# Halves for GpSimd, and thresholds on ScalarE, in a kernel of attention and two feed-forward blocks

## The chip, the cores and the metric

The kernel runs on one core of one Trainium2 chip. A core has five engines that work through queues of their own: TensorE (PE, matrix products and transposes into PSUM banks), VectorE (DVE), ScalarE (ACT), GpSimd (POOL) and SyncE (SP, which here issues nearly all transfers). Each queue is worked through in order; an instruction that needs a result of another engine waits at the head of its queue, and all behind it waits too. The metric is the time of one launch in microseconds (us) on the device; lower is better.

## The reference

```python
def _attn_ref(q, k, v, tau):                       # (4, 8, 576, 64) each
    scores = scale * np.matmul(q, k.transpose(0, 1, 3, 2))
    thresh = np.max(scores, axis=-1, keepdims=True) - tau
    scores = np.where(scores >= thresh, scores, -1000000000.0)
    scores = scores - np.max(scores, axis=-1, keepdims=True)
    attn = np.exp(scores)
    attn = attn / (np.sum(attn, axis=-1, keepdims=True) + 1e-09)
    return np.matmul(attn, v).astype(np.float32)
...
x = np.ascontiguousarray(attn_out.transpose(0, 2, 1, 3)).reshape(B * S, H * D)
h = x @ w_in                                       # 2304 x 512 by 512 x 2048
g = np.where(pos, h, np.where(neg, 0.0, (h + beta) ** 2 / (4.0 * beta)))
x = g @ w_out
h2 = x @ w_in2
return (h2 * np.clip(h2 + 3.0, 0.0, 6.0) / 6.0) @ w_out2
```

## The kernel before

**Attention.** The 32 heads are worked on in 16 jobs of two heads (four jobs for each of the four batches). A job has five blocks of queries: four of 128 rows, whose scores of the two heads fill two pairs of PSUM banks, and a last one of the 64 remaining rows of both heads. For a block, TensorE makes the scores (L328). VectorE copies them out of PSUM with their sign changed and takes the minimum of each row on the way (L341, `nm`); that frees the banks. ScalarE makes the exponential, one instruction for each head (L353, `e`). VectorE adds tau to the minima (L356, the threshold `th`, two columns, one in the last block) and multiplies `e` with the comparison against the threshold, summing on the way (L362, the mask). TensorE turns the masked block (L277), ScalarE copies the turned pieces out (L390, L393, L404, L408, `Gf` and `Gt`), and TensorE multiplies them with v (L426); ScalarE copies the product to `xu` (L432).

A job's sums are inverted on VectorE (L445, L446), written to DRAM and read back spread over the partitions (`rb`, L467 two large transfers, L469 two small ones). GpSimd then multiplies `xu` with `rb` (L481). Queries and keys of jobs 4 to 15 are turned on VectorE (L286, L302), and GpSimd scales the queries (L288, `qt`).

**Feed-forward products.** Each 32-bit operand is split into a high and a low part, so that each product takes three matrix products (L666, L728, L708). For the activations ScalarE copies the high part (L649 `xh`, L683 `gh`) and VectorE or GpSimd subtracts (L650 `xl`, L684 `gl`). For the weights, which arrive as 64-bit words, eight instructions on three engines make 32-bit values: ScalarE L118 and L121, GpSimd L122, VectorE L129 and L135, GpSimd L137 (an integer addition), ScalarE L139 (high part), GpSimd L141 (low part). All are 128 x 512.

**Order.** Once the first batch's four jobs are done, a generator deals out pieces of the first feed-forward block between the pieces of attention (`mode["att"]` is true as long as attention runs, `mode["mlp"]` from the first product on); the rest follows when attention has ended. The order in which instructions of one engine stand is not that of the code: the framework schedules the program by a timeline of its own, so another length or another engine of one instruction can move its neighbours. Waits are placed by the regions that are read and written: who reads only the first 256 columns of `xu` waits for the instruction that writes these.

Of the kernel before, what the change touches and what calls it, by code (L numbers as in the profile page):

```python
# [10 lines left out]
ACTF = mybir.ActivationFunctionType  # L11
ALU = mybir.AluOpType
U32 = mybir.dt.uint32
I32 = mybir.dt.int32
# [4 lines left out]
def kernel(  # L19
# [13 lines left out]
    V, S, G, T = nc.vector, nc.scalar, nc.gpsimd, nc.tensor  # L33
    NB, NH, SEQ, D = q.shape
# [29 lines left out]
    taus = const.tile([128, 4], F32, name="taus")  # L64
# [9 lines left out]
    def f32(ap):  # L74
        return ap.bitcast(F32)
# [26 lines left out]
    def after(ins, prev, sync=False):  # L102
        if prev is not None:
            kind = mybir.DependencyClass.Sync if sync else mybir.DependencyClass.NoSync
            why = mybir.DependencyReason.ANTI if sync else mybir.DependencyReason.DATA
            tc.add_manual_dep(ins.ins, prev.ins.name, mybir.DependencyInfo(kind, why), reason="pace")

    pe_pins = []
    pins = {"S": None, "V": None, "G": None}

    def split_a(kind, m, f):
        t = wraw.pop((kind, m, f))
        pool = wbase if f < NF1 else wpool[f]
        hi = pool.tile([128, 512], F32R, tag=f"w{kind}h{f}", name=f"w{kind}h{f}")
        lo = pool.tile([128, 512], F32R, tag=f"w{kind}l{f}", name=f"w{kind}l{f}")
        c = stage.tile([128, 512], U32, tag="w_c", name="w_c", bufs=2)
        r = t[:, :, 0].bitcast(I32)
        x = S.activation(out=r, in_=t[:, :, 0], func=ACTF.Copy, scale=2.0 ** -29)  # L118
        after(x, pins["S"])
        if mode["att"]:  # L120
            after(S.activation(out=f32(c), in_=f32(t[:, :, 1]), func=ACTF.Abs), x)  # L121
            G.tensor_scalar(  # L122
                out=f32(c), in0=f32(c), scalar1=122879.9921875, scalar2=2.0 ** -15, op0=ALU.min, op1=ALU.max)
        else:
            S.activation(out=f32(c), in_=f32(t[:, :, 1]), func=ACTF.Abs)
            x = V.tensor_scalar(
                out=f32(c), in0=f32(c), scalar1=2.0 ** -15, scalar2=122879.9921875, op0=ALU.max, op1=ALU.min)
            after(x, pins["V"])
        V.tensor_scalar(out=c, in0=c, scalar1=3, scalar2=0x3FFFFFFF,  # L129
                        op0=ALU.logical_shift_left, op1=ALU.bitwise_and)  # L130
        wc[kind, m, f] = (hi, lo, c, t, r)

    def split_b(kind, m, f):
        hi, lo, c, t, r = wc.pop((kind, m, f))
        V.scalar_tensor_tensor(out=c, in0=t[:, :, 1], scalar=0xC0000000, in1=c,  # L135
                               op0=ALU.bitwise_and, op1=ALU.bitwise_or)
        x = G.tensor_tensor(out=c.bitcast(I32), in0=c.bitcast(I32), in1=r, op=ALU.add)  # L137
        after(x, pins["G"])
        x = S.activation(out=hi, in_=f32(c), func=ACTF.Copy)  # L139
        after(x, pins["S"])  # L140
        x = G.tensor_tensor(out=lo, in0=f32(c), in1=f32(hi), op=ALU.subtract)  # L141
        after(x, pins["G"])
        wsp[kind, m, f] = (hi, lo)

    wc = {}
# [61 lines left out]
    mode = {"mlp": False, "att": True, "step": False, "t": 0, "s": 0, "n": 0}  # L207
# [4 lines left out]
    qt, kt = {}, {}  # L212
# [17 lines left out]
    def load_q(j):  # L230
        if j >= NJ:
            return
        E = nc.sync if j else nc.scalar
        b, hp = jobs[j]
        for h in HEADS:
            src = q[b, 2 * hp + h]
            if j >= JT:
                strips(qn, 0, src, h)
                continue
            E.dma_start(out=qn[:, 0:4, h * D:(h + 1) * D], in_=rows(src, b))  # L240
            E.dma_start(out=qn[0:TAIL, 4, h * D:(h + 1) * D], in_=src[MAIN:SEQ, :])
# [39 lines left out]
    def unit_q(j):  # L281
        if j >= NJ or j in qt:
            return
        qt[j] = ap.tile([128, SEQ], F32, tag="qt", name="qt", bufs=2)
        if j >= JT:
            V.transpose(out=qt[j], in_=qn.rearrange("p c n -> p (c n)")[:, 0:SEQ])  # L286
            load_q(j + 1)
            G.tensor_scalar(out=qt[j], in0=qt[j], scalar1=taus[:, 1:2], scalar2=None, op0=ALU.mult)  # L288
            return
        tm = unit_bank().rearrange("p e n -> p (e n)")  # L290
        for c in range(5):
            turn(tm[:, c * 128:(c + 1) * 128], qn[:, c, :], c == 0)
        load_q(j + 1)
        reads(S.activation(out=qt[j], in_=tm[:, 0:SEQ], func=ACTF.Copy, scale=taus[:, 1:2]))
# [52 lines left out]
    def em_exp(j, i, x):  # L347
        p, nm, th, es = blk[j, i]
        n = 1 if i == NBLK - 1 else 2
        if x >= n:  # L350
            return
        e = ap.tile([128, 2, HS], F32, tag="e", name="e", bufs=3)
        pins["S"] = S.activation(out=e, in_=p[:, x], func=ACTF.Exp, bias=nm[:, x:x + 1], scale=-1.0)  # L353
        es.append(e)
        if x == n - 1:
            V.tensor_scalar(out=th[:, 0:n], in0=nm[:, 0:n], scalar1=taus[:, 0:1], scalar2=None, op0=ALU.add)  # L356

    def em_mask(j, i):
# [112 lines left out]
    def em_norm(j):  # L471
        if j not in rbs:
            return
        while any(x[0] == j for x in pvq):
            pv_chunk()
        b, hp = jobs[j]
        rz, rb = rbs.pop(j)
        if j in OVER:
            load_v(j + 2)
            x = xu.pop(j)  # L480
            G.tensor_tensor(out=x, in0=x, in1=rb, op=ALU.mult)  # L481
            done_jobs.add(j)
            if b < NB - 1:
                nc.sync.dma_start(out=xd[b][:, hp, :], in_=x[:, 0:MAIN])
            nc.sync.dma_start(out=xd[NB][:, hp, b * TAIL:(b + 1) * TAIL], in_=x[:, MAIN:SEQ])
            return
        bm = unit_bank().rearrange("p e n -> p (e n)")
        for c in range(4):
            T.transpose(bm[:, c * 128:(c + 1) * 128], rb[:, c].rearrange("p h n -> p (h n)"), ident)
        load_v(j + 2)  # L490
        bt = bm[:, 512:640]
        T.transpose(bt, rz[:, 8, :].to_broadcast([128, 128]), ident)
        x = xu.pop(j)
        reads(V.tensor_tensor(out=x[:, 0:MAIN], in0=x[:, 0:MAIN], in1=bm[:, 0:MAIN], op=ALU.mult))
        done_jobs.add(j)
        if b < NB - 1:
            nc.sync.dma_start(out=xd[b][:, hp, :], in_=x[:, 0:MAIN])
        for h in HEADS:
            r = slice(64 * h, 64 * h + 64)
            reads(V.tensor_tensor(out=x[r, MAIN:SEQ], in0=x[r, MAIN:SEQ], in1=bt[r, 64 * h:64 * h + 64], op=ALU.mult))  # L500
        nc.sync.dma_start(out=xd[NB][:, hp, b * TAIL:(b + 1) * TAIL], in_=x[:, MAIN:SEQ])
# [288 lines left out]
    while o < len(outs):  # L790
        n = len(steps)
# [138 lines left out]
    for _ in attention():  # L930
# [11 lines left out]
        while credit > 0:  # L942
            c = next(part1)
# [98 lines left out]
```

## Time and profile before

| | |
|---|---|
| median of three runs | 1124.85 us (1124.29 to 1128.67) |
| the profiled execution | 1126.53 us, span 1124.7 us |
| granted TensorE clock in it | 0.994 of full speed |
| busy: PE, DVE, ACT, POOL | 1086.1, 586.9, 614.3, 435.5 us |
| chain that ended last | PE 86%, DVE 6%, ACT 3%, DMA 2% |

A profile shows one execution. Busy time is the union of an engine's instructions in a stretch; an instruction that waits for a port or a lock after it has started counts as busy. A row by lines has: line, engine, operation, output and inputs by the program's names with their shapes, number of instructions, then busy us and mean ns of one, then idle time of the engine before them and what ended it. A row of waits says who waited for whom, the sum in us, how often, and the longest. A row of the timeline has its start and length in us, and in brackets the idle time of the engine before it. `DVE_READ_ACCUMULATOR` rows belong to the instruction before them.

### The profile page before, as it was taken

Reading aid. Unit: us, or ns where it says so; the run is one execution under the profiler, and the core shown is the slowest. Engines: PE = TensorE matmul, PEld = TensorE weight load, DVE = VectorE, ACT = ScalarE, POOL = GpSimd, SP = SyncE. Lnnn points to the kernel's source line nnn. Section 1 sums busy time; section 2 is a strip of 40 time slices with the busy share of each in tenths; the row PEclk is TensorE's granted clock in tenths of the full one; section 3 lists DMA queues with packets and bytes.
Section 4 is the critical chain, followed back from the end, with each engine's and each line's share of the span. In section 5 each row is a group of like instructions: output and inputs, shape, how many; then the busy total and the mean of one; then the engine's idle time right before and its main releaser. Section 6 shows DMA issues by size and latency. Waiting matters only on the chain.

```text
span 1124.7 us, 17618 instructions
## 1 busy us (share of the span) xinstructions
PE 1086.1 (97%) x6478; PEld 881.8 (78%) x6478; DVE 586.9 (52%) x1204; ACT 614.3 (55%) x1215; POOL 435.5 (39%) x382
## 2 busy tenths in 40 slices
PE   7988779999999999999999999999999999999998
PEld 5555557778887778888889888888888888898886
DVE  5788979876666666256535855657410211211111
ACT  5677777776666666565657766645422322333222
POOL 1133667632212221246636666568622222222221
PEclk9999999999999999999999999999999999999999
DMA  6353535433222210015322444543110110010001
GB/s 166 95 117 79 135 102 157 121 73 87 63 59 64 55 39 24 12 49 169 94 85 85 132 147 153 153 128 102 35 38 1 34 38 1 10 38 6 14 1 38
DMA packets 140422, 84.26 MB, mean 75 GB/s; under 512 B 99632, under 2 KB 123440, under 8 KB 140336
## 3 DMA queue, kind: packets, MB, share of 16 engines
q1 hardware_dynamic: 138976, 82.84, 26.8%
q8 instruction: 51, 0.84, 0.3%
q10 hardware_dynamic: 1360, 0.30, 0.1%
q14 instruction: 35, 0.29, 0.1%
HBM read 65.73 MB, written 17.37 MB: 74 GB/s over the span
## 4 chain that ended last, share of the span: by engine, by line
PE 86%; DVE 6%; ACT 3%; DMA 2%; issue 1%; POOL 1%; SPq 1%; ACTq 0%; DVEq 0%; POOLq 0%
PE Q L666 35%; PE P L708 28%; PE Q L728 7%; PE P L328 6%; PE Q L426 5%; PE Q L277 5%; DVE p L341 2%; DVE p L362 2%; ACT e L353 1%; DMA qn<-in_q_dram 1%; DMA w_raw<-in_moe_w_in_dram 0%; DMA rb<-rd 0%; DVE w_c L135 0%; ACT Gf L390 0%; SPq L227 0%
## 5 line engine op out<-in xcount | busy, mean ns | idle before, releaser
L684 POOL TENSOR_TENSOR gl<-r,gh 128x512 fp32r<-128x512 f32 (+1 forms) x190 | 202.4, 1065 | 508.3 <-ACT gh L683 506.4
L666 PE MATMUL Q<-xh,wih 128*128 128x512 f32 (+1 forms) x760 | 262.7, 346 | 6.9 <-DVE r L677 6.0
L666 PE MATMUL Q<-xh,wil 128*128 128x512 f32 (+1 forms) x760 | 257.6, 339 | 0.0
L666 PE MATMUL Q<-xl,wih 128*128 128x512 f32 (+1 forms) x760 | 257.5, 339 | 0.0
L680 DVE SCALAR_TENSOR_TENSOR r<-r,Q 128x512 f32<-128x512 f32 (+1 forms) x80 | 50.7, 634 | 249.3 <-ACT r L679 249.2
L683 ACT ACTIVATE gh<-r 128x512 fp32r<-128x512 f32 (+1 forms) x190 | 99.9, 526 | 128.5 <-PE P L708 52.3
L666 PEld LDWEIGHTS Q<-xh,wih 128*128 128x128 f32 x760 | 144.6, 190 | 31.4 <-DVE r L677 8.2
L666 PEld LDWEIGHTS Q<-xl,wih 128*128 128x128 f32 x760 | 144.6, 190 | 15.8
L666 PEld LDWEIGHTS Q<-xh,wil 128*128 128x128 f32 x760 | 144.5, 190 | 15.3
L341 DVE TENSOR_SCALAR_CACHE_REDUCE p<-P 128x576 f32<-128x576 f32 x144 | 103.9, 751 | 54.4 <-PE Q L277 39.1
L362 DVE SCALAR_TENSOR_TENSOR p<-p,th,e 128x576 f32<-128x576 f32 x144 | 123.6, 879 | 15.4 <-ACT e L353 9.6
L679 ACT ACTIVATE r<-Q,three 128x512 f32<-128x512 f32 (+1 forms) x80 | 51.5, 643 | 143.7 <-PE Q L666 140.5
L353 ACT ACTIVATE e<-p,nm 128x576 f32<-128x576 f32 x144 | 108.5, 774 | 29.2 <-DVE p L341 28.3
L677 DVE SCALAR_TENSOR_TENSOR r<-r,Q 128x256 f32<-128x256 f32 (+1 forms) x110 | 54.9, 499 | 120.2 <-ACT r L676 117.0
L277 PE MATMUL Q<-ident,p 128*128 128x128 f32 x656 | 108.5, 284 | 7.8 <-ACT Gf L390 4.3
L328 PE MATMUL P<-kt,qt 64*128 64x288 f32 (+1 forms) x640 | 99.4, 429 | 14.7 <-DVE p L341 13.8
L708 PE MATMUL P<-woh,gh 128*128 128x512 f32 x288 | 111.9, 390 | 0.6 <-DVE ob L766 0.6
L708 PE MATMUL P<-wol,gh 128*128 128x512 f32 x288 | 112.2, 390 | 0.0
L708 PE MATMUL P<-woh,gl 128*128 128x512 f32 x288 | 111.0, 390 | 0.0
L277 PEld LDWEIGHTS Q<-ident,p 128*128 128x128 f32 x656 | 74.5, 142 | 44.2 <-issue 11.8
L137 POOL TENSOR_TENSOR w_c<-w_c,w_raw 128x512 int32<-128x512 int32 x64 | 88.7, 1387 | 41.7 <-DVE w_c L135 21.8
L390 ACT ACTIVATE Gf<-Q 128x512 f32<-128x512 f32 x128 | 74.2, 595 | 34.4 <-PE Q L277 33.6
(91 smaller groups left out, 1834.3 us busy)
## 6 DMA issues: line engine op xcount, KB each, us to landing
w_raw<-in_moe_w_in_dram SPq DMA_DIRECT2D x32, 512.0 KB
w_raw<-in_moe_w_out_dram SPq DMA_DIRECT2D x32, 512.0 KB
vn<-in_v_dram SPq DMA_DIRECT2D x32, 128.0 KB
x2p<-ob SPq DMA_DIRECT2D x16, 256.0 KB
x2d<-ob SPq DMA_DIRECT2D x16, 256.0 KB
xst<-x2d SPq DMA_DIRECT2D x16, 256.0 KB
out_dram<-ob SPq DMA_DIRECT2D x16, 256.0 KB
xst<-xd SPq DMA_DIRECT2D x15, 256.0 KB
```

Source lines behind the costliest of these rows:

```text
L137: x = G.tensor_tensor(out=c.bitcast(I32), in0=c.bitcast(I32), in1=r, op=ALU.add)
L277: x = T.transpose(out, in_, ident)
L328: mm = T.matmul(o, qt[j][r, c], kt[j][r, k0:k0 + HS], start=True, stop=True, skip_group_check=True)
L341: reads(V.tensor_scalar(out=p[:, x], in0=s[:, :, 0:HS], scalar1=-1.0, scalar2=3e38, op0=ALU.mult, op1=ALU.min, accum_out=nm[:, x:x + 1]), ...
L353: pins["S"] = S.activation(out=e, in_=p[:, x], func=ACTF.Exp, bias=nm[:, x:x + 1], scale=-1.0)
L362: V.scalar_tensor_tensor(out=p[:, x], in0=p[:, x], scalar=th[:, x:x + 1], in1=e, op0=ALU.is_le, op1=ALU.mult, accum_out=zt[j][:, z:z + 1])
L390: S.activation(out=f[:, h, :, d0:d0 + 128], in_=tm.rearrange("p (c n) -> p c n", c=4), func=ACTF.Copy)
L666: mm = T.matmul(h, l[:, kk * 128:(kk + 1) * 128], r, start=(x == 0), stop=(x == 3 * KD - 1))
L683: x = S.activation(out=gh, in_=r, func=ACTF.Copy)
L684: y = G.tensor_tensor(out=gl, in0=r, in1=f32(gh), op=ALU.subtract)
L708: T.matmul(a, l, r, start=(first and x == 0), stop=(last and x == 2))
L728: mm = T.matmul(o, l, r, start=(f == fs[0] and x == 0 and i == 0), stop=(f == fs[-1] and x == 2 and i == 1), skip_group_check=True)
```

## The change

Three things are changed. While attention runs, GpSimd's conversions of weights (L137 and L141), its scaling of the queries (L288) and its product of the result with the inverse sums (L481) are issued as two instructions on half of the columns each, instead of one; outside attention they stay whole. And in the jobs 0 to 6 the threshold is an addition on ScalarE (an Identity with tau as bias), issued after the first exponential of the block, instead of one on VectorE after the last. GpSimd's L122 and L684 are not changed. GpSimd has 66 instructions more; VectorE 35 fewer, ScalarE 35 more.

```diff
--- before.py
+++ after.py
@@ -108,6 +108,10 @@
     pe_pins = []
     pins = {"S": None, "V": None, "G": None}
 
+    def halves(n):
+        w = n // 2 if mode["att"] else n
+        return [slice(a, a + w) for a in range(0, n, w)]
+
     def split_a(kind, m, f):
         t = wraw.pop((kind, m, f))
         pool = wbase if f < NF1 else wpool[f]
@@ -134,12 +138,14 @@
         hi, lo, c, t, r = wc.pop((kind, m, f))
         V.scalar_tensor_tensor(out=c, in0=t[:, :, 1], scalar=0xC0000000, in1=c,
                                op0=ALU.bitwise_and, op1=ALU.bitwise_or)
-        x = G.tensor_tensor(out=c.bitcast(I32), in0=c.bitcast(I32), in1=r, op=ALU.add)
-        after(x, pins["G"])
+        for s in halves(512):
+            x = G.tensor_tensor(out=c.bitcast(I32)[:, s], in0=c.bitcast(I32)[:, s], in1=r[:, s], op=ALU.add)
+            after(x, pins["G"])
         x = S.activation(out=hi, in_=f32(c), func=ACTF.Copy)
         after(x, pins["S"])
-        x = G.tensor_tensor(out=lo, in0=f32(c), in1=f32(hi), op=ALU.subtract)
-        after(x, pins["G"])
+        for s in halves(512):
+            x = G.tensor_tensor(out=lo[:, s], in0=f32(c)[:, s], in1=f32(hi)[:, s], op=ALU.subtract)
+            after(x, pins["G"])
         wsp[kind, m, f] = (hi, lo)
 
     wc = {}
@@ -285,7 +291,8 @@
         if j >= JT:
             V.transpose(out=qt[j], in_=qn.rearrange("p c n -> p (c n)")[:, 0:SEQ])
             load_q(j + 1)
-            G.tensor_scalar(out=qt[j], in0=qt[j], scalar1=taus[:, 1:2], scalar2=None, op0=ALU.mult)
+            for s in halves(SEQ):
+                G.tensor_scalar(out=qt[j][:, s], in0=qt[j][:, s], scalar1=taus[:, 1:2], scalar2=None, op0=ALU.mult)
             return
         tm = unit_bank().rearrange("p e n -> p (e n)")
         for c in range(5):
@@ -352,7 +359,10 @@
         e = ap.tile([128, 2, HS], F32, tag="e", name="e", bufs=3)
         pins["S"] = S.activation(out=e, in_=p[:, x], func=ACTF.Exp, bias=nm[:, x:x + 1], scale=-1.0)
         es.append(e)
-        if x == n - 1:
+        if j < 7:
+            if x == 0:
+                S.activation(out=th[:, 0:n], in_=nm[:, 0:n], func=ACTF.Identity, bias=taus[:, 0:1])
+        elif x == n - 1:
             V.tensor_scalar(out=th[:, 0:n], in0=nm[:, 0:n], scalar1=taus[:, 0:1], scalar2=None, op0=ALU.add)
 
     def em_mask(j, i):
@@ -478,7 +488,8 @@
         if j in OVER:
             load_v(j + 2)
             x = xu.pop(j)
-            G.tensor_tensor(out=x, in0=x, in1=rb, op=ALU.mult)
+            for s in halves(SEQ):
+                G.tensor_tensor(out=x[:, s], in0=x[:, s], in1=rb[:, s], op=ALU.mult)
             done_jobs.add(j)
             if b < NB - 1:
                 nc.sync.dma_start(out=xd[b][:, hp, :], in_=x[:, 0:MAIN])
```

The scheduler moves neighbours with it. In the changed program line numbers are higher: L353 is L360, L362 is L372, L390 is L400, L404 is L414, L432 is L442, L649 is L660, L139 is L144; L341 is L348; L137, L141, L481, L288 and L684 are L142, L147, L492, L295 and L695; L122 and L129 are L126 and L133; the new threshold is L364.

ScalarE's queue around the high part of the first job's result (`xh`), before:

```order
L432 ACTIVATE xu<-Q_430 128x320
L390 ACTIVATE Gf<-Q_470 128x4x128
L390 ACTIVATE Gf<-Q_476 128x4x128
L404 ACTIVATE Gt<-Q_482 128x128
L353 ACTIVATE e<-p,nm 128x576
L390 ACTIVATE Gf<-Q_503 128x4x128
L390 ACTIVATE Gf<-Q_509 128x4x128
L404 ACTIVATE Gt<-Q_523 128x128
L353 ACTIVATE e<-p,nm 128x576
L139 ACTIVATE wih_342<-w_c 128x512
L649 ACTIVATE xh<-xu 128x256
L353 ACTIVATE e<-p,nm 128x576 x2
```

and in the changed program:

```order
L442 ACTIVATE xu<-Q_430 128x320
L400 ACTIVATE Gf<-Q_470 128x4x128
L400 ACTIVATE Gf<-Q_476 128x4x128
L414 ACTIVATE Gt<-Q_482 128x128
L660 ACTIVATE xh<-xu 128x256
L360 ACTIVATE e<-p,nm 128x576
L400 ACTIVATE Gf<-Q_503 128x4x128
L400 ACTIVATE Gf<-Q_509 128x4x128
L414 ACTIVATE Gt<-Q_523 128x128
L364 ACTIVATE th<-nm,taus 128x2
L360 ACTIVATE e<-p,nm 128x576
L144 ACTIVATE wih_342<-w_c 128x512
```

`xh` stands six instructions further up, right behind the first small copy (`Gt`); thresholds stand between the two exponentials of a block. It waits for the first half of the product alone (L492's first instruction, which waits for the two large transfers of `rb`). For the second job it is the same, for the third two instructions.

VectorE's queue in the first blocks of job 0, before:

```order
L341 TENSOR_SCALAR p,nm<-P_188 128x576
L341 TENSOR_SCALAR p,nm<-P_189 128x576
L356 TENSOR_SCALAR th<-nm,taus 128x2
L362 SCALAR_TENSOR_TENSOR p,z<-p,th,e 128x576 x2
L341 TENSOR_SCALAR p,nm<-P_207 128x576
L341 TENSOR_SCALAR p,nm<-P_208 128x576
L356 TENSOR_SCALAR th<-nm,taus 128x2
L362 SCALAR_TENSOR_TENSOR p,z<-p,th,e 128x576 x2
L341 TENSOR_SCALAR p,nm<-P_242 128x576
```

and in the changed program:

```order
L348 TENSOR_SCALAR p,nm<-P_188 128x576
L348 TENSOR_SCALAR p,nm<-P_189 128x576
L372 SCALAR_TENSOR_TENSOR p,z<-p,th,e 128x576 x2
L348 TENSOR_SCALAR p,nm<-P_207 128x576
L348 TENSOR_SCALAR p,nm<-P_208 128x576
L372 SCALAR_TENSOR_TENSOR p,z<-p,th,e 128x576 x2
L348 TENSOR_SCALAR p,nm<-P_242 128x576
```

The masks now stand directly behind the minima.

GpSimd's queue where the first products of the feed-forward block begin, before:

```order
L122 TENSOR_SCALAR w_c<-w_c 128x512 x2
L684 TENSOR_TENSOR gl<-r,gh 128x256
L137 TENSOR_TENSOR w_c<-w_c,w_raw 128x512
L481 TENSOR_TENSOR xu<-xu,rb 128x576
L137 TENSOR_TENSOR w_c<-w_c,w_raw 128x512
L141 TENSOR_TENSOR wil_1438<-w_c,wih_1437 128x512
L684 TENSOR_TENSOR gl<-r,gh 128x256
L141 TENSOR_TENSOR wol_1501<-w_c,woh_1500 128x512
L122 TENSOR_SCALAR w_c<-w_c 128x512
L288 TENSOR_SCALAR qt<-qt,taus 128x576
```

and in the changed program, from the same place:

```order
L126 TENSOR_SCALAR w_c<-w_c 128x512 x2
L142 TENSOR_TENSOR w_c<-w_c,w_raw 128x256 x2
L695 TENSOR_TENSOR gl<-r,gh 128x256
L492 TENSOR_TENSOR xu<-xu,rb 128x288 x2
L147 TENSOR_TENSOR wil_1453<-w_c,wih_1452 128x256 x2
L142 TENSOR_TENSOR w_c<-w_c,w_raw 128x256 x2
L126 TENSOR_SCALAR w_c<-w_c 128x512
L295 TENSOR_SCALAR qt<-qt,taus 128x288 x2
L695 TENSOR_TENSOR gl<-r,gh 128x256
L147 TENSOR_TENSOR wol_1518<-w_c,woh_1517 128x256 x2
```

The halves of one tile stand behind each other in all places shown; nothing was put between them. The scaling of the queries (`qt`) moved up past one low part of an activation and one of a weight; the first low part of a weight (`wil`) now stands ahead of the second addition.

## Rows read from the trace of the kernel before

**Rows 1.** stretches: engines' busy us in each, with instructions, TensorE's clock, DMA
```profile
0.00:9.00 9.00, 6.15 (x35) 5.54 (x35) 0.38 (x3) 2.84 (x4) 1.67 (x14) 1.00 0.44 96
9.00:105.00 96.00, 83.02 (x569) 50.95 (x571) 79.49 (x215) 68.24 (x141) 22.59 (x18) 0.96 0.53 124
105.00:190.00 85.00, 67.82 (x481) 50.31 (x481) 75.96 (x164) 65.89 (x142) 54.70 (x49) 0.96 0.46 116
190.00:470.00 280.00, 278.80 (x2178) 224.33 (x2177) 185.42 (x487) 187.95 (x417) 80.07 (x79) 1.00 0.26 64
470.00:1124.70 654.70, 650.29 (x3224) 550.67 (x3222) 245.68 (x336) 289.35 (x514) 276.50 (x223) 1.00 0.22 67
```

**Rows 2.** longest wait of TensorE, 0 to 190 us (us, times, longest)
```profile
PE P L328 <- DVE p L341: 13.8, 15, 2.7
```

**Rows 3.** VectorE's lines by form, 105 to 190 us
```profile
L362 DVE SCALAR_TENSOR_TENSOR p<-p,th,e 128x576 f32<-128x576 f32 x23 | 25.2, 1109 | 1.5 <-ACT e L353 1.1
L135 DVE SCALAR_TENSOR_TENSOR w_c<-w_raw,w_c 128x512 uint32<-128x512 uint32 x11 | 9.5, 868 | 0.1
L129 DVE TENSOR_SCALAR w_c<-w_c 128x512 uint32<-128x512 uint32 x11 | 7.3, 662 | 0.2 <-POOL w_c L122 0.2
L356 DVE TENSOR_SCALAR th<-nm,taus 128x2 f32<-128x2 f32 x10 | 4.1, 412 | 0.1
L356 DVE TENSOR_SCALAR th<-nm,taus 128x1 f32<-128x1 f32 x3 | 0.6, 190 | 0.0
```

**Rows 4.** the same; two rows of 300 to 470, two of 9 to 105
```profile
L362 DVE SCALAR_TENSOR_TENSOR p<-p,th,e 128x576 f32<-128x576 f32 x48 | 38.4, 817 | 5.5 <-ACT e L353 3.5
L356 DVE TENSOR_SCALAR th<-nm,taus 128x2 f32<-128x2 f32 x21 | 4.8, 228 | 0.7
L135 DVE SCALAR_TENSOR_TENSOR w_c<-w_raw,w_c 128x512 uint32<-128x512 uint32 x4 | 2.7, 686 | 0.0
L129 DVE TENSOR_SCALAR w_c<-w_c 128x512 uint32<-128x512 uint32 x4 | 1.7, 426 | 0.0
```

**Rows 5.** timeline, 169 to 172.6 us: GpSimd, then VectorE (start, us)
```profile
169.09 1.44 POOL L481 TENSOR_TENSOR xu<-xu,rb 128x576 f32<-128x576 f32 x1
170.48 1.47 POOL L141 TENSOR_TENSOR wol<-w_c,woh 128x512 fp32r<-128x512 f32 x1
169.16 1.66 DVE L129 TENSOR_SCALAR w_c<-w_c 128x512 uint32<-128x512 uint32 x1 [0.17 <-POOL w_c L122]
170.86 1.65 DVE L135 SCALAR_TENSOR_TENSOR w_c<-w_raw,w_c 128x512 uint32<-128x512 uint32 x1
```

**Rows 6.** GpSimd's lines by form, 850 to 1124 us
```profile
L684 POOL TENSOR_TENSOR gl<-r,gh 128x512 fp32r<-128x512 f32 x41 | 52.9, 1291 | 170.3 <-ACT gh L683 170.3
L684 POOL TENSOR_TENSOR gl<-r,gh 128x256 fp32r<-128x256 f32 x16 | 11.8, 737 | 34.5 <-ACT gh L683 34.5
```

**Rows 7.** timeline, 175 to 178 us: GpSimd, then VectorE
```profile
175.34 2.19 POOL L288 TENSOR_SCALAR qt<-qt,taus 128x576 f32<-128x576 f32 x1 [0.42 <-DVE qt L286]
176.64 0.78 DVE L362 SCALAR_TENSOR_TENSOR p<-p,th,e 128x576 f32<-128x576 f32 x1
```

**Rows 8.** ScalarE's lines by form, 9 to 105 us
```profile
L353 ACT ACTIVATE e<-p,nm 128x576 f32<-128x576 f32 x42 | 31.6, 774 | 18.5 <-DVE p L341 18.2
L390 ACT ACTIVATE Gf<-Q 128x512 f32<-128x512 f32 x36 | 20.1, 592 | 0.8 <-PE Q L277 0.7
L404 ACT ACTIVATE Gt<-Q 128x128 f32<-128x128 f32 x18 | 5.2, 286 | 0.0
```

**Rows 9.** the chain that ended last, 9 to 105 us: shares by line
```profile
by line: DVE p L341 16.7%; PE P L328 16.1%; PE Q L426 12.3%; PE Q L277 8.3%; DVE p L362 7.8%; DMA qn<-in_q_dram 5.7%; DMA rb<-rd 5.2%; issue 3.3%; ACT e L353 3.0%; POOL xu L481 2.9%; SPq L227 2.9%; DVE th L356 2.5%; PE P L277 1.6%; DVE kt L
```

**Rows 10.** timeline, 35.9 to 43.5 us: ScalarE, then GpSimd
```profile
35.98 0.30 ACT L404 ACTIVATE Gt<-Q 128x128 f32<-128x128 f32 x1
42.48 0.42 ACT L649 ACTIVATE xh<-xu 128x256 fp32r<-128x256 f32 x1 [2.73 <-POOL xu L481]
41.05 1.40 POOL L481 TENSOR_TENSOR xu<-xu,rb 128x576 f32<-128x576 f32 x1 [12.18 <-DMA rb<-rd]
```

## The prediction

> **What bounds the kernel now.** I read the stretches first [rows 1]. They cut the span into five: start, attention alone (9 to 105 us), attention with the first products of the feed-forward mixed in (105 to 190), the same mix later (190 to 470), products alone. The reader is to compare the length of each with TensorE's busy time. From 190 us on the engine misses 280.0 - 278.8 = 1.2 us and 654.7 - 650.3 = 4.4 us; what VectorE, ScalarE or GpSimd do there is covered. Before it misses 2.9, 13.0 and 17.2 us. These 33 us are all that any change on the other three engines can give back, and the kernel's end moves by what they move.
>
> Then the waits of TensorE up to 190 us [rows 2]: by far the longest in total, 13.8 us in 15 waits, is that of the scores for VectorE's line 341, which empties their banks. So VectorE's queue is late there. In 105 to 190 us it is busy 76.0 of 85 us [rows 1], the fullest engine. Part of that is no work: its lines by form show the mask (L362) at 1109 ns there [rows 3] and at 817 ns in 300 to 470 us, where GpSimd is quieter; L135, L129 and the threshold L356 are stretched too [rows 3, 4]. The timeline shows the cause [rows 5]: GpSimd's L481 runs from 169.09 for 1.44 us; VectorE's L129, issued at 169.16, ends 0.3 us after it, 1.66 us long instead of 0.43. L135 then waits for L141 in the same way. An instruction of VectorE that meets one of GpSimd stands until that has ended. The stretch in 105 to 190 us: L362 23 x (1109 - 817) = 6.7 us, L135 11 x (868 - 686) = 2.0, L129 11 x (662 - 426) = 2.6, L356 10 x (412 - 228) = 1.8, together 13.1 us.
>
> **The change part by part, between 105 and 190 us.** *Halves of the conversions (L137, L141) and of the product L481.* A GpSimd product of 512 columns takes 1291 ns undisturbed, of 256 columns 737 [rows 6]: 2.16 ns a column and 183 ns for each instruction. A half of 288 columns is then 0.81 us (an estimate from these rows). What a half saves VectorE I work out on [rows 5]. Now L129 loses 1.66 - 0.43 = 1.23 us and L135 1.65 - 0.69 = 0.96. In halves, L481's first part ends at 169.09 + 0.81 = 169.90, L129 ends 0.3 us later, at 170.2; the second part runs to 171.0 while L135 waits, and L135 ends near 171.5 instead of 172.5. Saved: 1.0 of 2.2 us, 45%. Where the next instructions of VectorE are all of the kind that waits, the second half only hands the stall on, and nothing is saved; where the next reads a score bank (L341), the second half is hidden. I take 40% of 13.1 us: -5.2 us. The ends are 0 (all handed on) and -9 (two thirds, nearly every second half hidden). GpSimd itself pays 24 extra instructions here (22 conversions and 2 products) x 0.183 = 4.4 us, and each second half may wait for VectorE once more. Its 85 - 54.7 = 30.3 us of idle time [rows 1] cover that; without cover it would be those 4.4 us, since ScalarE's L139 stands behind L137 and everything on ScalarE behind L139.
>
> *The scaling L288 in halves.* [Rows 7]: in 175.34 to 177.53 it runs 2.19 us, and the mask issued at 176.64 beside it takes 0.78 us, not stretched. So nothing is freed on VectorE; 0. The first scores of the next job need only the first half of the columns, so they may start up to half of 1.7 us earlier, but TensorE is held there by L341; 0 as well, with -1 as an end. The Trainium skill, SBUF — State Buffer, "Who interferes with whom", says of VectorE and GpSimd that whichever starts first holds the shared pair of ports for its whole instruction and that a vector instruction with two SBUF inputs contends with a GpSimd instruction that reads SBUF. [Rows 5] agree with it; [rows 7] do not, since L288 reads SBUF and the mask has two SBUF inputs. By that rule the halves of L288 would spare masks half of it, some 0.9 us for each of the three in this stretch, and the sum would be 2.7 us lower.
>
> *The thresholds of jobs 0 to 6 on ScalarE.* Of VectorE's ten wide thresholds in [rows 3] nine leave (the last is job 7's): 9 x 0.228 [rows 4] = 2.1 us, and the three narrow ones 3 x 0.19 = 0.6: -2.7 us together. Their stretch is in the 13.1. On ScalarE no row shows a two-column addition with a bias operand. Bounds: two plain copies [rows 8] give (592 - 286) / 384 = 0.80 ns a column and so 0.18 us for an empty one; the exponential with a bias operand gives 774 - 576 x 0.80 = 0.31 us. I take 0.30, since the bias is there: 12 x 0.30 = 3.6 us more on an engine that is busy 65.9 of 85 us [rows 1]. Behind each stands the second exponential of its block, and behind that the copies that free TensorE's banks; the first mask now waits for ScalarE too. I let a third of it reach the end: +1.2 us, ends 0 and +3.6.
>
> Sum of this stage: -5.2 - 2.7 + 1.2 = -6.7 us. TensorE is idle 17.2 us in it, so there is room for all of it, and after 190 us nothing waits that could give it back.
>
> **Between 9 and 105 us** 23 thresholds leave VectorE, but it is not full there (79.5 of 96 us). The chain has them at 2.5%, 2.4 us [rows 9]; in these places the mask follows its threshold at once and will now wait for one on ScalarE that takes as long: 0, ends -2.4 and +2. The other thing is ScalarE's queue. The high part of the first job's result (L649) waits 2.73 us for GpSimd's product at 41.05 [rows 10]. In the changed program it waits for the product's first half alone, which needs the two large transfers of the sums but not the small last one; but it also stands further up, right behind the copy that ended at 36.28 us, ahead of two exponentials, two large copies, a small one and a conversion. If the transfers land early, the wait and half of 1.40 us are saved; if they land when the product started, the queue stands from 36.3 to 41.05 + 0.81 = 41.9 with 3.5 us of work still behind it, and loses 3.5 - 0.6 = 2.9 us. The same twice more, the third time moved by two instructions only (0.8 us): ends -4.8 (all of its waits) and +6.6. The order of program and chip differ here, no row tells where between, so 0.
>
> **After 190 us** 0: TensorE is covered there [rows 1]. If the cover went, the rest of the 66 extra instructions, 27 (12 fall before 105 us, 3 scalings and 24 others in the stage), would cost 27 x 0.183 = 4.9 us.
>
> **Sum.** -6.7 us. The profiled execution took 1126.53 us (span 1124.7 and 1.8 around it) and would go to 1119.8; it lies 1.7 us above the median of the three runs, 1124.85, which would go to **1118.2 us**.
>
> **Rivals.** *The stall is only handed on.* For it: VectorE's kinds that wait come in rows of three or four (mask, mask, L135, L129), and GpSimd's too [rows 5]. Against: two score-bank readers in each block. Then only the thresholds count, -2.7 + 1.2 = -1.5: 1123.4 us.
>
> *ScalarE becomes the late engine, between 36 and 84 us.* The moved L649 blocks its queue three times (+6.6), and a third of 23 x 0.30 = 6.9 us of thresholds adds 2.3; with nothing from the port the stage after gives -1.5. 1124.85 + 6.6 + 2.3 - 1.5 = 1132.3 us. It decides as soon as the three waits together grow by more than 6.7 us and TensorE has no banks left to fill. For it: the chain goes through exactly this transfer and product, 5.2% and 2.9% [rows 9]. Against: the first half waits for less.
>
> *The halves run through.* If GpSimd's second half took the port before the waiting vector instruction, that would wait for both and 183 ns more: 24 x 0.18 = 4.4 us on top of -1.5, 1127.8 us. Against it stand [rows 5]: L141 follows directly on L481, yet L129 got in between, and L141 took 1.47 us.
>
> **How the numbers follow.** A measurement of this kernel can tell about 0.5%, 5.6 us, from no change. The forecast's own range is 1113 to 1122 us; chance 0.55, of which 0.45 below 1119.2 and 0.10 within the bound. Handed on 0.28, within. Late ScalarE 0.14, slower. Halves that run through 0.03, within. Faster 0.45, same 0.41, slower 0.14. The range for 8 in 10 takes in the first two whole and the near end of the third: 1111 to 1128.
>
> **What the profile will show.** Right: in the stage before TensorE fills, the mask's mean falls from 1109 to near 950 ns, TensorE's idle time from 17 to near 11 us; the halves of 256 columns near 0.75 us; thresholds on ScalarE near 0.30 us; GpSimd's idle time still over 20 us. Wrong: a mask still near 1100 ns (handed on); L649's three waits over 8 us together, or ScalarE among TensorE's longest waits (late ScalarE); idle time of TensorE after 190 us over 10 us.

## The result, and the profile after

The changed kernel takes **1136.33 us** (median of 4 runs, 1133.62 to 1136.98) against 1124.81 for the kernel before: a ratio of 1.0088, 95% interval 1.0064 to 1.0112. It is slower by about 10 us; the forecast was 1118.2, with 1128 as the upper end. The profiled execution took 1136.98 us, 1135.2 of them the span.

The stretches of the changed kernel, in the columns of [rows 1]:

```profile
9.00:105.00 96.00, 75.44 (x507) 46.52 (x509) 65.67 (x172) 66.08 (x147) 22.42 (x27) 0.93 0.48 113
105.00:190.00 85.00, 71.84 (x493) 49.38 (x489) 67.98 (x158) 68.48 (x156) 57.01 (x70) 0.94 0.44 108
190.00:470.00 280.00, 277.67 (x2138) 223.50 (x2138) 194.40 (x498) 188.90 (x418) 92.82 (x112) 0.99 0.28 70
470.00:1135.20 665.20, 660.52 (x3309) 559.60 (x3308) 246.14 (x342) 295.78 (x527) 278.29 (x227) 1.00 0.21 66
```

Between 105 and 190 us TensorE is idle 85 - 71.8 = 13.2 us, 4.0 less than before: this stage gained. Between 9 and 105 it is idle 20.6 us instead of 13.0, and its mean granted clock is 0.93 there instead of 0.96. Over the whole span TensorE's busy time, from the first part of the pages, shows a second loss beside the idle one:

```profile
PE 1092.0 (96%) x6478; PEld 885.0 (78%) x6478; DVE 574.6 (51%) x1169; ACT 621.6 (55%) x1250; POOL 452.2 (40%) x448
```

The kernel before has 1086.1 us for the same 6478 matmuls. So 6.0 of the 10.5 us by which the span grew are matmuls that ran longer, and 4.5 are idle time.

In the rows that follow, of the lines not yet named, L335 is the scores (L328 before), L283 the turning (L277), L436 the product with v (L426) and L661 the low part `xl` (L650). The waits of TensorE in 9 to 105 us (us in total, times, longest), first two of the kernel before, then three of the changed kernel:

```profile
PE P L328 <- DVE p L341: 6.8, 10, 1.5
PE Q L426 <- ACT Gf L390: 1.6, 1, 1.6
...
PE P L335 <- DVE p L348: 9.6, 8, 3.1
PE Q L436 <- ACT Gf L400: 4.9, 1, 4.9
PE Q L283 <- ACT Gf L400: 3.1, 5, 1.0
```

What stands out is one wait of 4.9 us for a copy of ScalarE; the longest of its kind before was 1.6. The timeline of ScalarE around it (start, us, in brackets the idle time before and what ended it):

```profile
62.84 0.30 ACT L414 ACTIVATE Gt<-Q 128x128 f32<-128x128 f32 x1
67.94 0.42 ACT L660 ACTIVATE xh<-xu 128x256 fp32r<-128x256 f32 x1 [4.81 <-POOL xu L492]
68.27 0.76 ACT L360 ACTIVATE e<-p,nm 128x576 f32<-128x576 f32 x1
68.93 1.06 ACT L400 ACTIVATE Gf<-Q 128x512 f32<-128x512 f32 x2
```

GpSimd, VectorE and TensorE in the same stretch:

```profile
67.12 1.54 POOL L492 TENSOR_TENSOR xu<-xu,rb 128x288 f32<-128x288 f32 x2 [11.48 <-DMA rb<-rd]
```

```profile
68.39 0.55 DVE L661 TENSOR_TENSOR xl<-xu,xh 128x256 fp32r<-128x256 f32 x1 [4.51 <-ACT xh L660]
```

```profile
63.94 1.24 PE L335 MATMUL P<-kt,qt 64*128 64x288 f32 x8
70.05 3.68 PE L436 MATMUL Q<-Gf,vn 128*64 128x256 f32 x16 [4.87 <-ACT Gf L400]
```

Read from the bottom: TensorE ends its scores at 65.2 and needs the copies L400; ScalarE has them in its queue, but behind L660, the high part of the second job's result; that waits for GpSimd's product, and this for the transfer of the sums. VectorE stands at L661 for the same result, so three engines wait for one transfer, though no matrix product uses xh before 123.8 us. At the first job's xh it is VectorE's queue that holds TensorE: the minimum that frees the banks of the scores (L348) stands behind `xl`, and TensorE waits 3.08 us for it. The kernel before had both minima of that block done before its `xl`.

```profile
41.19 0.55 DVE L661 TENSOR_TENSOR xl<-xu,xh 128x256 fp32r<-128x256 f32 x1 [2.31 <-ACT xh L660]
41.67 0.74 DVE L348 TENSOR_SCALAR_CACHE_REDUCE p<-P 128x576 f32<-128x576 f32 x1
42.47 1.81 PE L335 MATMUL P<-kt,qt 64*128 64x288 f32 x6 [3.08 <-DVE p L348]
```

ScalarE's three waits for the product, in the changed kernel and in the kernel before:

```profile
ACT xh L660 <- POOL xu L492: 7.9, 3, 4.8
...
ACT xh L649 <- POOL xu L481: 4.8, 3, 2.7
```

What follows on TensorE after the gap at 65.2 us is in short stretches of the same run (columns as above):

```profile
60.00:65.00 5.00, 4.73 (x36) 3.30 (x34) 3.47 (x10) 3.11 (x7) 0.00 (x0) 1.00 0.54 163
65.00:70.00 5.00, 0.18 (x2) 0.00 (x0) 0.55 (x1) 2.06 (x5) 1.54 (x2) 0.86 0.45 99
70.00:75.00 5.00, 4.95 (x23) 2.67 (x24) 4.62 (x11) 4.55 (x10) 1.60 (x3) 0.50 0.08 24
75.00:80.00 5.00, 4.47 (x35) 3.31 (x35) 2.94 (x8) 3.21 (x8) 2.00 (x3) 0.96 0.26 43
```

After 4.87 us of standing still the granted clock is 0.50, the lower of its two levels (1.2 GHz), for about 5 us. A matmul of 128x256 takes 641 ns there; a wider one, 128x320, takes 445 ns between 50 and 60 us at 1.00:

```profile
L436 PE MATMUL Q<-Gf,vn 128*64 128x256 f32 x16 | 3.7, 641 | 4.9 <-ACT Gf L400 4.9
...
L436 PE MATMUL Q<-Gf,vn 128*64 128x320 f32 x16 | 2.6, 445 | 0.0
```

The other large wait is VectorE's, for the thresholds on ScalarE, which the kernel before has on VectorE; in the changed kernel first between 9 and 105, then between 105 and 190 us:

```profile
DVE p L372 <- ACT th L364: 12.1, 17, 1.6
...
DVE p L372 <- ACT th L364: 7.1, 7, 1.7
```

### The profile page after: what moved, and what is told of

Same layout as the page of the kernel before. It is cut to its first block, busy times and chain, and to the rows that moved or that the text cites. A ratio compares the mean times of both kernels' runs of the same rounds, so it can differ in the third digit from the quotient of the medians.

```text
span 1135.2 us, 17665 instructions
## 1 busy us (share of the span) xinstructions
PE 1092.0 (96%) x6478; PEld 885.0 (78%) x6478; DVE 574.6 (51%) x1169; ACT 621.6 (55%) x1250; POOL 452.2 (40%) x448
## 4 chain that ended last, share of the span: by engine, by line
PE 85%; ACT 3%; DVE 3%; DMA 3%; POOL 3%; issue 1%; SPq 1%; ACTq 0%; DVEq 0%; POOLq 0%
PE Q L677 34%; PE P L719 28%; PE Q L739 7%; PE Q L436 6%; PE P L335 6%; PE Q L283 5%; DMA rb<-rd 1%; DVE p L348 1%; ACT e L360 1%; DVE p L372 1%; POOL w_c L142 1%; ACT Gf L400 1%; DMA qn<-in_q_dram 1%; POOL gl L695 1%; POOL wol L147 0%
## 5 line engine op out<-in xcount | busy, mean ns | idle before, releaser
L695 POOL TENSOR_TENSOR gl<-r,gh 128x512 fp32r<-128x512 f32 (+1 forms) x190 | 202.0, 1064 | 501.9 <-ACT gh L694 499.9
L677 PE MATMUL Q<-xh,wih 128*128 128x512 f32 (+1 forms) x760 | 262.1, 345 | 1.4 <-DVE r L688 1.4
L677 PE MATMUL Q<-xh,wil 128*128 128x512 f32 (+1 forms) x760 | 257.2, 338 | 0.0
L677 PE MATMUL Q<-xl,wih 128*128 128x512 f32 (+1 forms) x760 | 257.2, 338 | 0.0
L677 PEld LDWEIGHTS Q<-xh,wih 128*128 128x128 f32 x760 | 144.3, 190 | 25.4 <-issue 4.4
L677 PEld LDWEIGHTS Q<-xl,wih 128*128 128x128 f32 x760 | 144.3, 190 | 15.7
L677 PEld LDWEIGHTS Q<-xh,wil 128*128 128x128 f32 x760 | 144.2, 190 | 15.3
L372 DVE SCALAR_TENSOR_TENSOR p<-p,th,e 128x576 f32<-128x576 f32 x144 | 123.0, 873 | 28.1 <-ACT th L364 19.2
L348 DVE TENSOR_SCALAR_CACHE_REDUCE p<-P 128x576 f32<-128x576 f32 x144 | 104.5, 751 | 60.5 <-PE Q L283 39.6
L360 ACT ACTIVATE e<-p,nm 128x576 f32<-128x576 f32 x144 | 109.9, 773 | 35.3 <-DVE p L348 34.7
L283 PE MATMUL Q<-ident,p 128*128 128x128 f32 x656 | 106.7, 283 | 12.3 <-ACT Gf L400 7.3
L335 PE MATMUL P<-kt,qt 64*128 64x288 f32 (+1 forms) x640 | 99.6, 430 | 14.1 <-DVE p L348 11.1
L283 PEld LDWEIGHTS Q<-ident,p 128*128 128x128 f32 x656 | 74.0, 142 | 47.8 <-ACT Gf L400 14.9
L142 POOL TENSOR_TENSOR w_c<-w_c,w_raw 128x512 int32<-128x512 int32 (+1 forms) x84 | 92.4, 1109 | 35.1 <-DVE w_c L139 18.4
L400 ACT ACTIVATE Gf<-Q 128x512 f32<-128x512 f32 x128 | 74.1, 595 | 35.1 <-PE Q L283 34.3
```

The costliest lines, as they stand in the source:

```text
L142: x = G.tensor_tensor(out=c.bitcast(I32)[:, s], in0=c.bitcast(I32)[:, s], in1=r[:, s], op=ALU.add)
L283: x = T.transpose(out, in_, ident)
L335: mm = T.matmul(o, qt[j][r, c], kt[j][r, k0:k0 + HS], start=True, stop=True, skip_group_check=True)
L348: reads(V.tensor_scalar(out=p[:, x], in0=s[:, :, 0:HS], scalar1=-1.0, scalar2=3e38, op0=ALU.mult, op1=ALU.min, accum_out=nm[:, x:x + 1]), ...
L372: V.scalar_tensor_tensor(out=p[:, x], in0=p[:, x], scalar=th[:, x:x + 1], in1=e, op0=ALU.is_le, op1=ALU.mult, accum_out=zt[j][:, z:z + 1])
L400: S.activation(out=f[:, h, :, d0:d0 + 128], in_=tm.rearrange("p (c n) -> p c n", c=4), func=ACTF.Copy)
```

## The experiments

Every kernel is timed in five rounds beside the kernel before; the ratio is to that kernel, with its 95% interval. Three edits are combined. **H** is the halves, **T** the thresholds on ScalarE, as in the diff of the change. **X** holds xh (L660) of the first three jobs behind a given exponential of ScalarE; before, it stood behind the 15th, 24th and 32nd, in the changed kernel behind the 13th, 22nd and 31st:

```diff
         es.append(e)
+        exps.append(pins['S'])
...
-            S.activation(out=hi, in_=src, func=ACTF.Copy)
+            x = S.activation(out=hi, in_=src, func=ACTF.Copy)
+            if g == 0 and ph == 1 and kk < 3 and m == 0:
+                after(x, exps[(15, 24, 32)[kk] - 1])
```

In the place of (15, 24, 32) other numbers are named where they are used. The few added lines move the line numbers by 1 to 4: L348 is L349, L372 is L369, L371 or L374.

In the profiled executions X is a narrow edit: between the changed kernel and the same with X, GpSimd's instructions stand in the same order, and on ScalarE, VectorE and TensorE only some that start before 105 us have changed places, `xh` and `xl` among them.

**The place of xh: four kernels.** Theory A: xh's new place makes the loss. B: the thresholds on ScalarE. C: the halves themselves.

Changed kernel with X:

> The changed kernel with one order added: ScalarE's xh of the first three jobs not before the exponential that it followed in the kernel before (15th, 24th, 32nd). Theory A: xh's three waits fall from 7.9 to under 4 us together and the time to 1122 to 1127 us. Theory B: still 1132 us or more, since the thresholds are untouched. Theory C: still 1132 or more.

Changed kernel with X, at (41, 41, 41):

> The changed kernel with xh of the first three jobs not before the 41st exponential, near 100 us, where all of their products are long done: no wait of ScalarE for GpSimd's product is left. Theory A: the lowest of the four, 1115 to 1122 us. Theories B and C: 1130 us or more.

H without T:

```diff
-        if j < 7:
-            if x == 0:
-                S.activation(out=th[:, 0:n], ...)
-        elif x == n - 1:
+        if x == n - 1:
```

> Halves everywhere, all thresholds back on VectorE. ScalarE's xh of the first two jobs stands 1 and 2 exponentials earlier than before (14th and 22nd instead of 15th and 24th). Theory A (the loss comes from the place of xh in ScalarE's queue): about 1130 us, two of the three waits of xh still long. Theory B (the masks wait for thresholds on ScalarE): faster than before, near 1120 us, since no threshold is there. Theory C (the halves themselves cost): 1134 us or more.

T without H (`halves(...)` replaced by one whole slice in all four places):

> Thresholds of jobs 0 to 6 on ScalarE, no halves anywhere. xh stands where it stands in the changed kernel (13th, 22nd, 31st exponential). Theory A: the loss stays or grows, 1135 to 1140 us, since xh now waits for the whole product too. Theory B: 1135 to 1140 us as well, masks behind their threshold. Theory C: back to about 1125 us.

Measured: after_pin **1123.45 us** (0.9992, 0.9983 to 1.0001), after_late 1125.72 (1.0011, 1.0002 to 1.0020), h_only 1134.09 (1.0082, 1.0069 to 1.0095), th_only 1151.11 (1.0237, 1.0216 to 1.0257). An order that moves three copies of 0.42 us takes back the whole loss: A; B and C had expected 1132 us or more of after_pin. The other three did not come out as A had it: after_late was not the lowest, h_only is what C expected (1134 or more) and not A's 1130, and th_only is 11 us above the ranges of both A and B. H and T alone are therefore taken up again below with xh held, as a second and a third pair that differ in X only: h_only 1134.09 against h_pin 1123.15, th_only 1151.11 against th_pin 1139.36. The first speaks against C, since the same halves lose nothing once xh is held. As ratios the place of xh costs 1.0% in the changed kernel, 1.0% with H and 1.1% with T, that is 11 to 12 us. Waits for product xu are gone from ScalarE's list, and the stretches of after_pin (9 to 105, 105 to 190 us) show where the time came from:

```profile
9.00:105.00 96.00, 79.78 (x582) 50.31 (x583) 73.67 (x193) 74.55 (x166) 24.99 (x30) 1.00 0.53 125
105.00:190.00 85.00, 69.60 (x487) 50.12 (x484) 70.51 (x155) 68.35 (x156) 61.52 (x73) 0.96 0.48 121
```

TensorE's busy sum fell from 1092.0 to 1083.1 us and its idle time from 43.1 to 39.1, at a mean granted clock of 0.996 instead of 0.986: in this pair of executions two thirds of the difference is clock. It is not a fixed share: with H alone busy time makes 6.1 of 11.4 us (1091.6 against 1085.5), with T alone 5.3 of 8.8 (1091.3 against 1086.0).

The same from the other side: the product xu alone in halves, which moves xh up (14th, 22nd, 31st). It is not as narrow as X: other instructions of ScalarE, VectorE, GpSimd and TensorE change places too, up to 240 us.

```diff
-            G.tensor_tensor(out=x, in0=x, in1=rb, op=ALU.mult)
+            for s in halves(SEQ):
+                G.tensor_tensor(out=x[:, s], in0=x[:, s], in1=rb[:, s], op=ALU.mult)
```

> The kernel before with the product xu in halves and nothing else (14 extra instructions). By that alone xh moves up in ScalarE's queue (behind the 14th, 22nd and 31st exponential instead of the 15th, 24th and 32nd). Theory A (place of xh): 1129 to 1137 us. Theory C (extra GpSimd work): the two halves cost 14 x 0.18 = 2.5 us at most, so 1124 to 1127 us.

Measured: **1131.57 us** (1.0058, 1.0045 to 1.0071): in the range of A, by 14 extra instructions, though without a run of this kernel with xh held. Its waits of ScalarE and TensorE, 9 to 105 us:

```profile
ACT xh L657 <- POOL xu L489: 7.6, 3, 3.7
```

```profile
PE Q L433 <- ACT Gf L397: 7.1, 3, 3.5
```

**What halves and thresholds are worth with xh held.**

H + X:

> Halves everywhere, thresholds on VectorE, xh of the first three jobs held behind the 15th, 24th and 32nd exponential. If the thresholds on ScalarE cost what the halves gain (VectorE's masks wait 5 to 7 us for them between 105 and 190 us): 1117 to 1121 us, clearly below the changed kernel with the same hold (1123.45). If the halves give nothing and the thresholds nothing: 1124 to 1126 us. If the thresholds are a gain: above 1126 us.

T + X:

> Thresholds of jobs 0 to 6 on ScalarE, no halves, xh held at the same places. If the place of xh was all that made the kernel with thresholds alone 1151 us: 1122 to 1127 us. If the thresholds cost by themselves (masks that wait for them): 1129 us or more.

H + X, and T for jobs 4 to 6 only (`if 4 <= j < 7`):

> Halves everywhere, xh held, thresholds on ScalarE for jobs 4 to 6 only (where VectorE was the fullest engine). If the thresholds of jobs 0 to 3 cost TensorE idle time between 9 and 105 us (16.2 us with them, 13.0 before) while those of jobs 4 to 6 pay: 1117 to 1121 us. If none matters: 1123 us. If those of jobs 4 to 6 are the costly ones: as with all of them, 1123, while the kernel with all on VectorE is lower.

Only the two conversions in halves (L137 and L141 of before), no X needed:

> Halves of the two conversions alone (40 of the 66 extra instructions); nothing else changed, and xh stands where it stood before without being held. By the prediction's term for the halves (40% of 13.1 us): 1119 to 1121 us. If the second half only hands the stall on: 1124. If the extra 183 ns of each cost: 1127 or more.

Measured: h_pin 1123.15 us (0.9985, 0.9975 to 0.9995), th_pin **1139.36** (1.0128, 1.0111 to 1.0146), th46_pin 1123.10 (0.9986, 0.9977 to 0.9995), cv_only 1123.73 (0.9997, 0.9985 to 1.0008). So the halves gain 0.15%, the conversions alone nothing that can be told, where the prediction's term for them had 1119 to 1121; h_pin, too, lies between the ranges that it was given. In cv_only TensorE's idle time in 105 to 190 us did fall, from 17.2 to 13.1 us, but between 190 and 470 us it grew from 1.2 to 3.7, and the matmuls of the whole run took 1.9 us longer. Beside the halves the thresholds change nothing; without them they cost 1.3%: B holds there, and only there. VectorE's lines by form in h_pin, 105 to 190 us, against [rows 3]:

```profile
L371 DVE SCALAR_TENSOR_TENSOR p<-p,th,e 128x576 f32<-128x576 f32 x22 | 22.2, 1030 | 2.0 <-ACT e L361 1.6
...
L140 DVE SCALAR_TENSOR_TENSOR w_c<-w_raw,w_c 128x512 uint32<-128x512 uint32 x11 | 10.4, 949 | 0.2
L134 DVE TENSOR_SCALAR w_c<-w_c 128x512 uint32<-128x512 uint32 x11 | 6.0, 542 | 0.0
L689 DVE SCALAR_TENSOR_TENSOR r<-r,Q 128x256 f32<-128x256 f32 x11 | 4.5, 413 | 6.5 <-ACT r L688 6.5
...
L365 DVE TENSOR_SCALAR th<-nm,taus 128x2 f32<-128x2 f32 x9 | 2.8, 308 | 0.1
```

The stretch by the prediction's own sum is now 22 x (1030 - 817) + 11 x (949 - 686) + 11 x (542 - 426) + 9 x (308 - 228) = 4.7 + 2.9 + 1.3 + 0.7 = 9.6 us instead of 13.1. The mask and L134 lost less, L140 lost more: part of the stall may only have been handed on. VectorE, busy 70.6 of 85 us, is no longer full and waits 6.5 us for ScalarE at L689 (L677 before).

**Where the thresholds cost.** T + X with the conversions in halves; then no halves, with T for jobs 4 to 6 (`if 4 <= j < 7`) or 0 to 3 (`if j < 4`):

> Thresholds of jobs 0 to 6 on ScalarE, the conversions in halves, product and scaling whole, xh held. With all halves this was 1123.45 us, with none 1139.4. If the conversions are what the thresholds on ScalarE need (VectorE's masks, pushed later by the threshold, then meet a GpSimd instruction of 0.7 instead of 1.3 us): 1122 to 1128 us. If it is the scaling of the queries (VectorE and the first scores wait for it): 1133 us or more.

> No halves, xh held, thresholds on ScalarE for jobs 4 to 6 only. If the cost lies where masks meet whole GpSimd instructions (105 to 260 us): 1134 to 1139 us. If it lies in the stage before (longer way from reduction to mask, in which TensorE's idle time is 17 instead of 13 us): 1124 to 1128 us.

> No halves, xh held, thresholds on ScalarE for jobs 0 to 3 only. The other way round: 1126 to 1130 us if the cost lies after 105 us (only the 4 us more of idle time before it are left), 1135 us or more if it lies before.

Measured: cv_th_pin 1127.49 us (1.0022, 1.0014 to 1.0031), th46_whole_pin 1138.22 (1.0106, 1.0089 to 1.0123), th03_whole_pin 1132.94 (1.0065, 1.0053 to 1.0077). Both groups cost, and together (1139.36) little more than jobs 4 to 6 alone; the last measurement lies between its two ranges. In th03_whole_pin VectorE waits between 9 and 105 us for thresholds:

```profile
DVE p L374 <- ACT th L366: 13.4, 15, 1.9
```

and TensorE is idle 17.0 us there instead of 13.0. In T + X the stretches 105 to 190 and 190 to 265 us, and in the same kernel L134 in these 160 us:

```profile
105.00:190.00 85.00, 64.66 (x433) 45.45 (x429) 71.04 (x140) 60.73 (x139) 49.09 (x43) 0.92 0.41 103
190.00:265.00 75.00, 68.05 (x518) 54.24 (x519) 57.20 (x132) 53.31 (x120) 37.92 (x36) 1.00 0.39 104
```

```profile
L134 DVE TENSOR_SCALAR w_c<-w_c 128x512 uint32<-128x512 uint32 x16 | 14.4, 902 | 2.3 <-POOL w_c L127 2.2
```

TensorE is idle 20.3 and 7.0 us; with the conversions in halves it is 14.7 and 2.6, and L134's mean is 728 ns. TensorE's busy sum in T + X is that of the kernel before (1086.0 against 1086.1 us), so what the thresholds cost there is idle time and not clock, and halves of the conversions take back most of it. With jobs 4 to 6 alone (th46_whole_pin) 5.2 of the 13.3 us are busy time, so that does not hold for each of these kernels. Why a threshold that comes later meets whole conversions so much worse than halves I have not settled: the schedule of all engines differs between these kernels as well.

**The best place, and finer pieces.** H + X at (41, 41, 41); X at (41, 41, 41) alone; H + X at (20, 29, 38):

> Halves everywhere, thresholds on VectorE, xh of the first three jobs behind the 41st exponential. If ScalarE's wait at xh still costs something at the held places (1.4 us in the trace): 1120 to 1122 us. If these three copies, put at 100 us, now stand in the way of the first products of the feed-forward (2.3 us for the changed kernel, 1125.72 against 1123.45): 1124 to 1126 us.

> The kernel before with xh of the first three jobs behind the 41st exponential, nothing else. ScalarE's three waits there (4.8 us in the trace) go. If they cost TensorE what they last: 1120 to 1122 us. If other work filled them: 1124 to 1126 us.

> Halves everywhere, thresholds on VectorE, xh of the first three jobs five or six exponentials further back than held (behind the 20th, 29th and 38th): behind its product by some 10 us, and still well before 100 us. If the wait at xh's held place (1.4 us in the trace) is what separates 1123.15 from 1121.48: 1120 to 1122 us. If that difference is another schedule: 1122.5 us or more.

Measured: h_late 1121.48 us (0.9970, 0.9958 to 0.9982), before_late 1126.30 (1.0011, 1.0002 to 1.0019), **h_mid 1121.56** (0.9966, 0.9953 to 0.9978). H + X at (20, 29, 38) beats both kernels, by 0.3% and by 1.2% (0.9966 / 1.0088). The wait at xh's held place, 1.4 us, is about what separates it from h_pin (0.9985); that the one is the cause of the other is not shown. Without halves the move to the late place is worth nothing, though 4.8 us of waits go. Other work may have filled them, or the late place may cost what they gave back, as it does in the changed kernel (1125.72 against 1123.45); no run tells these two apart.

H + X at (20, 29, 38) with conversions in quarters, and with gl (L695) in halves too:

```diff
-        w = n // 2 if mode["att"] else n
+        w = n // (4 if n == 512 else 2) if mode["att"] else n
```

```diff
-        y = G.tensor_tensor(out=gl, in0=r, in1=f32(gh), op=ALU.subtract)
+        for s in halves(n):
+            y = G.tensor_tensor(out=gl[:, s], in0=r[:, s], in1=f32(gh)[:, s], op=ALU.subtract)
```

> As the kernel with xh behind the 20th, 29th and 38th exponential, thresholds on VectorE and halves (1121.56 us), but the two conversions in quarters of 128 columns (80 more GpSimd instructions while attention runs). If the stall at the port is still what bounds 105 to 190 us: 1118 to 1120 us. If it no longer is, or the pieces hand it on: 1121 to 1123 us. If 80 x 0.18 = 15 us more GpSimd work in all now shows: 1124 us or more.

> The same, conversions in halves, and the low part of the feed-forward's activations (gl) in halves too while attention runs. If the stall is still the bound: 1118 to 1120 us; if not: 1121 to 1123 us.

Measured: q_mid 1126.35 us (0.9999, 0.9985 to 1.0012), gl_mid 1125.11 (1.0002, 0.9991 to 1.0014). The gain is gone in both. gl_mid lies above both of its ranges, and why stays open. In q_mid the mask's mean falls to 924 ns between 105 and 190 us, but TensorE now waits 4.9 us for GpSimd's own result L148 (L141 before), a wait that h_mid does not have and the kernel before has with 0.5 us:

```profile
L371 DVE SCALAR_TENSOR_TENSOR p<-p,th,e 128x576 f32<-128x576 f32 x23 | 20.8, 924 | 3.4 <-ACT e L361 3.0
```

```profile
PE Q L740 <- POOL wol L148: 4.9, 4, 2.1
PE P L336 <- DVE p L349: 3.5, 3, 1.5
```

## Why the prediction was wrong

**The step that failed** is the one on 9 to 105 us: xh "stands further up", "ends -4.8 (all of its waits) and +6.6", "so 0". Measured, its place costs 11 to 13 us (as ratios 1.0088 against 0.9992; as medians 1136.33 against 1123.45), where the upper end was 6.6. I had the mechanism, as the rival "ScalarE becomes the late engine" with 0.14, and its sign was named rightly there: the wait for ScalarE's L400 stands second in TensorE's list. But that rival was to decide only if the three waits grew by more than 6.7 us, and they grew from 4.8 to 7.9; the first and the third even shrank (2.73 to 2.00 and 1.89 to 1.10 us), and the second grew from 0.19 to 4.81. So the length of ScalarE's waits was the wrong measure, for two reasons. I priced ScalarE's queue alone, while VectorE's xl moved up with xh: it held VectorE's queue for 8.4 us in all instead of 4.0, and at the first job TensorE waited 3.08 us for the minimum behind it. How much of the loss either queue makes by itself no run shows, since X moves both. And I left out TensorE's clock: the profiled executions of the changed kernel and of after_pin are 13.0 us apart, and 8.9 of these are matmuls that ran longer. [Rows 1] had a sign of that, a clock of 0.96 in both early stages, which I did not read. Taking 0 between ends so far apart was the wrong choice as well: most of the growth came from one late landing (the product of the second job started at 67.12 us), and that is no average of both ends.

**The halves.** -5.2 us was forecast in the stage. With thresholds on VectorE and xh held, TensorE's idle time there falls from 17.2 to 13.7 us (h_pin), 3.5 us, as much as the 13.1 - 9.6 us of stretch saved: 27% instead of 40%. The whole run gains only 0.15%, 1.7 us; TensorE's idle time between 190 and 470 us grows from 1.2 to 2.8. So the mask and L134 did get shorter, but the share was too high, and "after 190 us nothing waits that could give it back" did not hold. Halves of the conversions alone show it best: 4.1 us less idle time in the stage, and no gain in the run (cv_only). The two rows of h_pin, in the columns of [rows 1]:

```profile
105.00:190.00 85.00, 71.26 (x508) 53.72 (x505) 70.57 (x161) 65.94 (x145) 64.92 (x77) 0.96 0.51 131
190.00:470.00 280.00, 277.19 (x2153) 222.00 (x2154) 184.07 (x482) 186.95 (x415) 86.85 (x104) 1.00 0.24 60
```

**The thresholds.** 0.292 us was measured for the 0.30 I worked out. -2.7 + 1.2 in the stage was wrong: with halves they change nothing (1123.45 against 1123.15), without them they cost 14 us. Against what VectorE saves stands the masks' wait for ScalarE, 7.1 us in 7 waits. The trace shows how it comes about: a threshold needs the reductions of both columns, and on VectorE it followed the second at once (at 30.55 us in the kernel before, the reduction having ended at 30.50); on ScalarE one ran at 32.88 us in the changed kernel, 1.25 us after its second reduction (30.88 to 31.63 us), behind four copies:

```profile
31.74 0.64 ACT L403 ACTIVATE Gf<-Q 128x256 f32<-128x256 f32 x2
32.40 0.45 ACT L418 ACTIVATE Gt<-Q 64x64 f32<-64x64 f32 x2
32.88 0.29 ACT L364 ACTIVATE th<-nm,taus 128x2 f32<-128x2 f32 x1
```

"the mask follows its threshold at once and will now wait for one on ScalarE that takes as long: 0" overlooked the queue in between.

Added up, as ratios: some 11 us for the place of xh, -1.7 for the halves, nothing for the thresholds; that makes 9 of the 10 us measured.

**What held.** VectorE's instruction gets in between GpSimd's pieces, and the halves did not run through: in the changed kernel a mask issued at 139.56 us ended at 140.84, after the first half of a low part (L147, 138.98 to 140.22) and ahead of the end of the second (141.43). The prices: halves of 128x256 take 804 ns (L142) to 950 ns (L147, `wil`) on average between 105 and 190 us, stalls included, and near 735 where nothing stalls them. The scaling's halves: in the changed kernel masks beside them keep their length or nearly so (0.77 to 0.90 us), as [rows 7] said and against the Trainium skill, SBUF — State Buffer, "Who interferes with whom", by which a GpSimd instruction that reads SBUF contends with a mask of two SBUF inputs. Other schedules are less clear: in h_pin masks beside the scaling took up to 1.05 us while no other GpSimd instruction ran, so when the scaling holds a mask up and when not stays open. Products alone after 470 us: idle 4.7 us against 4.4, covered as forecast.

## What to carry to other kernels

Where a framework orders the program by its own timeline, a change of length or engine can move an instruction that it does not touch; look in the new order for instructions that have moved ahead of their late producer, and price everything behind them on every engine whose queue holds such an instruction. A copy that is needed much later is best held by an added order behind its producer. Compare also the whole run and not one stage: a stage that loses 4 us of TensorE's idle time can hand it to the next, as here. Add to the price of a TensorE gap of several us the slower clock that can follow it.

## What the runs showed of the hardware that was not expected

One gap of 4.87 us on TensorE was followed by some 5 us at a granted clock of 0.50 (the 1.2 GHz level). The Trainium skill, TensorE: Matmul & The Clock Gate, "Part 1: The HAM clock gate", has the array go to half rate when it idles and back when it is busy; the trace agrees. A long gap is not needed for it: in the changed kernel the mean clock was 0.64 between 190 and 195 us, and no wait of TensorE in the 5 us ahead was longer than 0.9 us. In each of the three pairs that differ in X only, holding xh shortened TensorE's busy time for the same 6478 matmuls: 1092.0 to 1083.1 us (changed kernel), 1091.6 to 1085.5 (H), 1091.3 to 1086.0 (T). Held xh alone does not make it short: th46_whole_pin has xh held and 1091.3 us.
